# Attention followed by two feed-forward stages: one VectorE instruction for maximum and bias, and the low half of the weights on VectorE

## The chip, the cores and the metric

The kernel runs on one core of one Trainium2 chip. The metric is the device time of one execution in microseconds. Engines are TensorE (PE; its weight loads are PEld), VectorE (DVE), ScalarE (ACT), GpSimd (POOL) and SyncE (SP), which issues most of the transfers.

## The reference, cut to what matters

For each of 4 batches and 8 heads (576 positions, head size 64) q and k are rotated, and then

```python
scores = scale * np.matmul(q_rot, k_rot.transpose(0, 1, 3, 2))
scores = scores - np.max(scores, axis=-1, keepdims=True)
attn = np.exp(scores)
attn = attn / (np.sum(attn, axis=-1, keepdims=True) + 1e-09)
return np.matmul(attn, v).astype(np.float32)
```

The result, 2304 rows of 512, goes through a feed-forward layer (`g = max(0.01 h, h)` between two matrices, 2048 wide), and then each row through one of eight experts (1024 wide, relu), chosen by the largest of eight scaled scores and weighted with its softmax value.

## The kernel before, in words

Products that need more than 16 bits are made of two parts, a high and a low one. For the softmax weights that means: an exponential E in 32 bits, its high part in 16 bits (`a_hi`), and the rest, E minus the high part, again in 16 bits (`a_lo`). Both parts lie side by side in the tile P, which one DMA transposes into PT for the product with v (`a_transpose`, `a_pv`).

Attention is cut into 144 units: 16 pairs of heads, 9 units in each (128 rows of one head; the ninth takes the last 64 rows of both heads). The program is written as a list of steps, one unit entering per step, and the order of all work is the order in which it is issued: each engine takes its instructions in that order. In step i the kernel issues the exponentials of unit i-1, maximum and bias of unit i, high and low part of unit i-1, the scores of unit i+1, and the product with v of unit i-4 (LAG is 4). The same step issues one part of the first feed-forward layer when one is due: `m_s1` and `m_s2` on TensorE, and between them `m_g` (ScalarE), `m_leaky` (VectorE), `m_gh` (ScalarE) and `m_gl` (GpSimd). Then there are pieces of other jobs: decoding the feed-forward matrices, which come as 64-bit numbers (`weights`, `decode`), preparing q, k and v of the next pair (`prep`, `prep_v`), and passing on finished rows (`x_done`, `route`). How many pieces a step takes is set by the planned costs in RATE1 to RATE3, not by time.

The order inside a step is a string of letters. ORDER1 holds until the first part of the feed-forward layer, ORDER2 while matrices are still being decoded beside it, ORDER3 after that:

```python
ORDER1 = 'EXFHfsBLSVGAKhlCx2s'
ORDER2 = 'ESVXsFfGHLAKhlC2xBs'
ORDER3 = 'FESXfHsLGVBKAshlC2x'
```

E is `a_exp`, X `a_max`, B `a_bias`, H `a_hi`, L `a_lo` with the transposing DMA, V `a_pv`, A its evacuation (`a_evac`), F and f `a_fin`, C `a_scores`, S `m_s1`, G `m_g`, K `m_leaky`, h `m_gh`, l `m_gl`, 2 `m_s2`, s and x pieces of other jobs.

Buffers: scores S two (`psS`), E two, P three, PT four, and one each for the feed-forward layer's PSUM tile h (`psH`) and for g. So the next `m_s1` can begin only when `m_leaky` (L279) has read h.

While matrices are being decoded, `a_hi` is an instruction of ScalarE (L528) and `a_bias` too (L515); after that both are VectorE's (L530, L517). `a_max` (L509) is VectorE's and `a_lo` (L534) GpSimd's throughout. After attention come the rest of the feed-forward layer, the choice of experts and the experts' blocks (`e_h`, `e_o`); the diff does not reach them.

Of the kernel before, what the change touches and what calls it, by code (L numbers as in the profile page):

```python
# [9 lines left out]
F32 = mybir.dt.float32  # L10
# [5 lines left out]
AF = mybir.ActivationFunctionType  # L16
ALU = mybir.AluOpType
AX = mybir.AxisListType
# [3 lines left out]
B, H, S, D = 4, 8, 576, 64  # L22
# [4 lines left out]
NBLK = NCH + NE - 1  # L27
NA = NCH - 2
NALWAYS = NCH + 2
LN_P = 10.397207708399179  # L30
EPS_P = 1e-9 * 32768.0
OOB = 8192
LAG = 4
XTB = 2
# [10 lines left out]
CAP = 1.5  # L45
TLOAD = 4
BUR = 1.5
ORDER1 = 'EXFHfsBLSVGAKhlCx2s'
ORDER2 = 'ESVXsFfGHLAKhlC2xBs'
ORDER3 = 'FESXfHsLGVBKAshlC2x'  # L50
SLIM = 1.2
ELOAD = 2
NMERGED = 60
# [48 lines left out]
def attention_moe_kernel(ctx: ExitStack, tc: tile.TileContext, qkv, w_in, w_out, emb, tau, w1, w2,  # L102
                         rope, ident, tokc, iota, pcol, out):
    nc = tc.nc

    def pool(name, bufs=1, **kw):
        return ctx.enter_context(tc.tile_pool(name=name, bufs=bufs, **kw))

    const = pool("const")
    small = pool("small", 3)  # L110
# [14 lines left out]
    enT = const.tile([128, 4, NE], F32, name="enT")  # L125
    junk = const.tile([128, 640], BF16, name="junk")
    itau = const.tile([128, 1], F32, name="itau")
    lnp = const.tile([128, 1], F32, name="lnp")
    half = const.tile([128, 1], F32, name="half")

    def ps_o():
# [43 lines left out]
    xjobs, vjobs, rjobs, wjobs = deque(), deque(), deque(), []  # L175
# [79 lines left out]
    def m_s1(i=None):  # L255

        if not m_ready() or i is not None and not pace(i):
            return None
        j, fs = munits[M.unit]
        M.unit += 1  # L260
        m = Ctx()
        m.j, m.fs, m.h = j, fs, ps_h()
        for f, c0, c1 in fs:
            n = 0
            for a, b_ in ((0, 0), (1, 0), (0, 1)):
                for c in range(4):
                    nc.tensor.matmul(m.h[:, c0:c1], lhsT=wi[:, a, c, 128 * f:128 * f + 128], rhs=xT[j][:, 4 * b_ + c, 0:c1 - c0],  # L267
                                     start=(n == 0), stop=(n == 11))
                    n += 1
        return m  # L270

    def m_g(m):
        m.g = mp.tile([128, 256], F32, name="g", bufs=1)
        for f, c0, c1 in m.fs:
            nc.scalar.activation(out=m.g[:, c0:c1], in_=m.h[:, c0:c1], func=AF.Copy, scale=uw[:, f:f + 1])  # L275

    def m_leaky(m):
        for f, c0, c1 in m.fs:
            nc.vector.scalar_tensor_tensor(out=m.g[:, c0:c1], in0=m.h[:, c0:c1], scalar=uw01[:, f:f + 1], in1=m.g[:, c0:c1], op0=ALU.mult, op1=ALU.max)  # L279
# [75 lines left out]
    pep = at.enter_context(tc.tile_pool(name="pep", bufs=2))  # L355
# [5 lines left out]
    pairs = {}  # L361
# [143 lines left out]
        return ps  # L505

    def a_max(g, u, ps):
        mx = small.tile([128, 2], F32, name="amx")
        nc.vector.tensor_reduce(out=mx[:, 0:1], in_=ps[:, :, 0:288], axis=AX.XY, op=ALU.max)  # L509
        return ps, mx  # L510

    def a_bias(g, u, ps, mx):
        sc = pairs[g][2]
        if any(z.live for z in wjobs):
            nc.scalar.activation(out=mx[:, 1:2], in_=mx[:, 0:1], func=AF.Identity, scale=sc[:, 1:2], bias=lnp)  # L515
        else:
            nc.vector.tensor_scalar(out=mx[:, 1:2], in0=mx[:, 0:1], scalar1=sc[:, 1:2], scalar2=LN_P, op0=ALU.mult, op1=ALU.add)  # L517

    def a_exp(g, u, ps, mx):
        sc = pairs[g][2]  # L520
        e = pep.tile([128, S], F32, name="E")
        nc.scalar.activation(out=e.rearrange("p (a b) -> p a b", a=2), in_=ps[:, :, 0:288], func=AF.Exp, scale=sc[:, 0:1], bias=mx[:, 1:2])  # L522
        return e

    def a_hi(e, i):
        p = pep.tile([128, 2 * S], F16, name="P", bufs=3)
        if i % (HI_ACT if M.unit else HI_A1) == 0 and any(z.live for z in wjobs):
            nc.scalar.activation(out=p[:, 0:576], in_=e, func=AF.Copy)  # L528
        else:
            nc.vector.tensor_copy(out=p[:, 0:576], in_=e)  # L530
        return p

    def a_lo(e, p):
        nc.gpsimd.tensor_tensor(out=p[:, 576:1152], in0=e, in1=p[:, 0:576], op=ALU.subtract)  # L534

    def a_transpose(p):
        pt = ptp.tile([128, 9, 128], F16, name="PT")
        nc.sync.dma_start_transpose(out=pt, in_=p)
        return pt
# [19 lines left out]
    def merged(g, u):  # L559
        return 9 * g + u < NMERGED  # L560

    def a_evac(g, u, o, xo):
        w = 65 if merged(g, u) else 129
        for h, q0, m, ob, oc in pv_parts(g, u):
            nc.scalar.activation(out=xo[ob:ob + m, h, 0:w], in_=o[ob:ob + m, oc:oc + w], func=AF.Copy)  # L565

    def a_fin(g, u, xo):
# [11 lines left out]
        w = 64 if merged(g, u) else 128  # L579
        nc.vector.tensor_scalar(out=rd[r], in0=xo[r, :, w:w + 1], scalar1=EPS_P, scalar2=s3[r, 2:3], op0=ALU.add, op1=ALU.mult)  # L580
        yield
# [71 lines left out]
    nc.sync.dma_start(out=idn, in_=ident)  # L653
    nc.sync.dma_start(out=itau, in_=tau.to_broadcast([128, 1]))
    nc.vector.memset(ones, 2.0)
    nc.vector.memset(lnp, LN_P)
    nc.vector.memset(half, -0.5)
    for i in range(2):
        nc.gpsimd.memset(v16s[i][:, 0:5, :, 128:130], 1.0)
# [74 lines left out]
    def end(g):  # L734
        for _ in g:
            pass
# [235 lines left out]
    units = [(g, u) for g in range(4 * B) for u in range(9)]  # L972
    n = len(units)
    ps_, pt_, xo_ = {}, {}, {}
# [13 lines left out]
    def slot(x=False, must=False):  # L988
        used = dict(A=0.0, V=0.0, G=0.0)
        for z in jobs():  # L990
            p = z.nxt
            if p.x != x or M.step < p.at or M.tick < p.tick or (p.when is not None and not p.when()):
                continue
            if x and L.x == M.tick:
                continue
            if p.must != must:
                continue
            if not p.must and z in wjobs and any(budget[e] <= 0 for e in p.cost):
                continue
            if not p.must and any(used[e] >= SLIM for e in p.cost):  # L1000
                continue
            for e, c in p.cost.items():
                budget[e] -= c
                used[e] += c
            if x:
                L.x = M.tick
            z.begun = True
            z.run()

    def step(i):  # L1010

        M.tick += 1
        M.step = i if i is not None else M.step
        rate = RATE1 if M.unit == 0 else RATE2 if any(z.live for z in wjobs) else RATE3
        for e in budget:
            budget[e] = min(budget[e] + rate[e], BUR * rate[e])
        now = i is not None and 0 <= i < n
        prv = i is not None and 0 <= i - 1 < n
        fin = i is not None and 0 <= i - LAG < n
        slot(must=True)  # L1020
        m = f = None
        for z in ORDER1 if rate is RATE1 else ORDER2 if rate is RATE2 else ORDER3:
            if z == "E" and prv:
                e = a_exp(*units[i - 1], *ps_.pop(i - 1))
            elif z == "S":
                m = m_s1(i)
            elif z == "X" and now:
                ps_[i] = a_max(*units[i], ps_[i])
            elif z == "F" and L.fin and i is not None:
                f = a_fin(*L.fin)  # L1030
                next(f)
                L.fin = None
            elif z == "f" and f:
                end(f)
            elif z == "B" and now:
                a_bias(*units[i], *ps_[i])
            elif z == "H" and prv:
                p = a_hi(e, i)
            elif z == "L" and prv:
                a_lo(e, p)  # L1040
                pt_[i - 1] = a_transpose(p)
            elif z == "V" and fin:
                g, u = units[i - LAG]
                o = a_pv(g, u, pt_.pop(i - LAG))
            elif z == "A" and fin:
                if u % 2 == 0:
                    xo_[g, u // 2] = pep.tile([128, 2, 129], F32, name="xo")
                a_evac(g, u, o, xo_[g, u // 2])
                if u % 2 or u == 8:
                    L.fin = (g, u, xo_.pop((g, u // 2)))  # L1050
            elif z == "G" and m:
                m_g(m)
            elif z == "K" and m:
                m_leaky(m)
            elif z == "h" and m:
                m_gh(m)
            elif z == "l" and m:
                m_gl(m)
            elif z == "C" and i is not None and 0 <= i + 1 < n:
                ps_[i + 1] = a_scores(*units[i + 1])  # L1060
            elif z == "2" and M.q:
                m_s2(M.q.popleft())
            elif z == "x":
                slot(x=True)
            elif z == "s":
                slot()
        if m:
            M.q.append(m)
        if R.late:
            slot()  # L1070
            slot()
# [85 lines left out]
    for i in range(4):  # L1157
# [17 lines left out]
                            in1=cend.unsqueeze(1).to_broadcast([1, NBLK, NE]), op=ALU.is_ge)  # L1175
# [27 lines left out]
    g = gates(0, NCH)  # L1203
# [103 lines left out]
```

## Time and profile before

| | |
|---|---|
| median of 3 runs | 1080.92 us (1079.94 to 1080.98) |
| the profiled execution | 1080.7 us, of which the span is 1078.9 us |
| TensorE busy | 956.0 us (89%) |
| VectorE busy | 790.2 us (73%) |
| ScalarE busy | 716.5 us (66%) |
| GpSimd busy | 563.3 us (52%) |
| `a_max` L509 | 144 instructions, 107.7 us |
| `a_lo` L534 | 144 instructions, 204.3 us |
| `a_exp` L522 | 144 instructions, 118.2 us |

The span runs from the first to the last instruction. A share over the whole span mixes stages with different limits, so the stages are looked at one by one. A mean duration well above an instruction's shortest one means that it was held while it ran.

### The profile page before, as it was taken

The numbers are of one execution on the slowest core, as the hardware profiler recorded it, in microseconds if no ns is written. First come the engines' busy times: TensorE is split into PE (matmuls) and PEld (weight loads), VectorE is DVE, ScalarE is ACT, GpSimd is POOL, SyncE is SP. The second block draws the span as 40 slices with busy tenths as digits, with TensorE's granted clock in tenths as the row PEclk, the third lists the DMA queues.
The fourth block names the chain that finished last, engine by engine and source line by source line (L and its number), as shares of the span: only waits on it lengthen the run. The fifth ranks groups of instructions, "written<-read, shape, count | busy, mean of one in ns | idle before, by whom it ended". The sixth has DMA issues, their size and how long they took to land. (4 is left out here: it accounts for less than half of the span.)

```text
span 1078.9 us, 19752 instructions
## 1 busy us (share of the span) xinstructions
PE 956.0 (89%) x6737; PEld 710.9 (66%) x6737; DVE 790.2 (73%) x1472; ACT 716.5 (66%) x1404; POOL 563.3 (52%) x558
## 2 busy tenths in 40 slices
PE   1666666988999999999998999999999899999996
PEld 1333333765667767677776677788877678888885
DVE  7898899886798763776976855312376999998992
ACT  7988888987556635455664554435345888888883
POOL 2577756776678663786777756422232361211111
PEclk9999999998999999999999999999999999999999
DMA  8979987965868853388588474301152111115190
GB/s 227 197 181 203 221 179 165 209 142 126 171 95 140 185 108 71 73 152 168 86 163 150 89 120 81 60 16 40 30 176 98 40 59 40 50 50 195 34 340 21
DMA packets 273611, 133.54 MB, mean 124 GB/s; under 512 B 244951, under 2 KB 253399, under 8 KB 273504
## 3 DMA queue, kind: packets, MB, share of 16 engines
q1 hardware_dynamic: 270304, 122.24, 52.0%
q0 software_dynamic: 3200, 9.97, 2.8%
q8 instruction: 55, 0.90, 0.3%
q14 instruction: 52, 0.43, 0.1%
HBM read 120.04 MB, written 10.49 MB: 121 GB/s over the span
## 5 line engine op out<-in xcount | busy, mean ns | idle before, releaser
L534 POOL TENSOR_TENSOR P<-E,P 128x576 f16<-128x576 f32 x144 | 204.3, 1419 | 63.7 <-DVE P L530 29.5
L267 PE MATMUL h<-xT,wi 128*128 128x256 f16 (+1 forms) x1920 | 216.7, 265 | 20.5 <-DVE g L279 12.1
L267 PEld LDWEIGHTS <-wi 128*128 128x128 f16 x1920 | 168.7, 100 | 64.4 <-issue 47.0
L287 POOL TENSOR_TENSOR gl<-g,gh 128x256 fp32r<-128x256 f32 x144 | 119.5, 830 | 147.3 <-ACT gh L283 141.5
L298 PE MATMUL acc<-wo,gh 128*128 128x512 f32 x576 | 196.4, 422 | 0.0
L279 DVE SCALAR_TENSOR_TENSOR g<-h,uw,g 128x256 f32<-128x256 f32 (+1 forms) x160 | 71.2, 453 | 141.0 <-ACT g L275 138.8
L275 ACT ACTIVATE g<-h,uw 128x256 f32<-128x256 f32 (+1 forms) x160 | 70.2, 449 | 136.8 <-PE h L267 117.5
L555 PE MATMUL o<-v,PT 128*128 128x65 f16 (+3 forms) x1770 | 102.8, 215 | 42.9 <-ACT xo L565 32.4
L555 PEld LDWEIGHTS <-PT 128*128 128x128 f16 (+1 forms) x1770 | 93.4, 111 | 55.6 <-issue 39.0
L503 PE MATMUL S<-stk 128*128 128x288 f16 (+1 forms) x320 | 105.4, 329 | 26.7 <-ACT E L522 25.7
L522 ACT ACTIVATE E<-S,amx,sc 128x576 f32<-128x576 f32 x144 | 118.2, 821 | 4.8 <-DVE amx L517 4.0
L283 ACT ACTIVATE gh<-g 128x256 fp32r<-128x256 f32 x144 | 60.0, 417 | 84.2 <-DVE g L279 83.6
L298 PE MATMUL acc<-wo,gl 128*128 128x512 f32 x288 | 115.6, 401 | 0.1
L298 PEld LDWEIGHTS acc<-wo,gh 128*128 128x128 f32 x576 | 98.5, 191 | 26.1 <-issue 0.2
L509 DVE TENSOR_REDUCE amx<-S 128x1 f32<-128x576 f32 x144 | 107.7, 748 | 1.4 <-PE S L504 1.1
L944 POOL DMA_INDIRECT out<-eo,idi x18 | 25.7, 1430 | 154.1 <-ACT eo L942 153.4
L504 PE MATMUL S<-stk 64*128 64x288 f16 (+1 forms) x320 | 105.9, 331 | 0.0
L504 PEld LDWEIGHTS <-stk 64*128 64x128 f16 (+1 forms) x320 | 31.2, 98 | 86.3 <-issue 64.4
L391 POOL TENSOR_TENSOR t<-raw,tab 128x320 f32<-128x320 f32 x62 | 64.1, 1054 | 7.4 <-DMA raw<-in_qkv 7.4
L530 DVE CAST P<-E 128x576 f16<-128x576 f32 x90 | 50.9, 565 | 19.9 <-ACT E L522 18.9
L298 PEld LDWEIGHTS acc<-wo,gl 128*128 128x128 f32 x288 | 54.9, 191 | 14.1 <-POOL gl L287 1.5
L426 DVE SCALAR_TENSOR_TENSOR stg<-raw,ps,stg 128x320 f16<-128x320 f32 x64 | 57.7, 941 | 0.0
(239 smaller groups left out, 1956.5 us busy)
## 6 DMA issues: line engine op xcount, KB each, us to landing
rb<-in_w SPq DMA_DIRECT2D x78, 512.0 KB
ra<-in_w SPq DMA_DIRECT2D x76, 512.0 KB
raw<-in_qkv SPq DMA_DIRECT2D x15, 640.0 KB
raw<-in_w_in SPq DMA_DIRECT2D x16, 512.0 KB
raw<-in_w_out SPq DMA_DIRECT2D x16, 512.0 KB
raw<-in_qkv SPq DMA_DIRECT2D x18, 320.0 KB
x2s<-x SPq DMA_DIRECT2D x18, 256.0 KB
v<-v SPq DMA_DIRECT2D x16, 162.5 KB
```

The costliest lines, as they stand in the source:

```text
L267: nc.tensor.matmul(m.h[:, c0:c1], lhsT=wi[:, a, c, 128 * f:128 * f + 128], rhs=xT[j][:, 4 * b_ + c, 0:c1 - c0], start=(n == 0), stop=(n == ...
L275: nc.scalar.activation(out=m.g[:, c0:c1], in_=m.h[:, c0:c1], func=AF.Copy, scale=uw[:, f:f + 1])
L279: nc.vector.scalar_tensor_tensor(out=m.g[:, c0:c1], in0=m.h[:, c0:c1], scalar=uw01[:, f:f + 1], in1=m.g[:, c0:c1], op0=ALU.mult, op1=ALU.max)
L287: nc.gpsimd.tensor_tensor(out=m.gl, in0=m.g, in1=m.gh.bitcast(F32), op=ALU.subtract)
L298: nc.tensor.matmul(M.acc[t], lhsT=g_[:, tt], rhs=wo[:, a, f], start=(f == 0 and n == 0), stop=(f == NF - 1 and n == 2))
L391: eng.tensor_tensor(out=t2[t][:, :, :, o:o + 32], in0=raw[:, t, :, :, i:i + 32], in1=sn[:, :, o:o + 32].unsqueeze(1).to_broadcast([128, 2, ...
L503: nc.tensor.matmul(ps[o:o + m, n, 0:288], lhsT=stk[:, h, c0:c0 + m], rhs=stk[:, 2 + h, ks], start=True, stop=False)
L504: nc.tensor.matmul(ps[o:o + m, n, 0:288], lhsT=stk[hr, h, c0:c0 + m], rhs=stk[hr, 4, ks], start=False, stop=True)
L509: nc.vector.tensor_reduce(out=mx[:, 0:1], in_=ps[:, :, 0:288], axis=AX.XY, op=ALU.max)
L522: nc.scalar.activation(out=e.rearrange("p (a b) -> p a b", a=2), in_=ps[:, :, 0:288], func=AF.Exp, scale=sc[:, 0:1], bias=mx[:, 1:2])
L534: nc.gpsimd.tensor_tensor(out=p[:, 576:1152], in0=e, in1=p[:, 0:576], op=ALU.subtract)
L555: nc.tensor.matmul(o[ob:ob + m, oc + z:oc + z + w], lhsT=pt[:, i, q0:q0 + m], rhs=v16[:, i, h, c:c + w], start=(n == 0), stop=(n == len(to ...
```

## The change

Maximum and bias become one VectorE instruction: it multiplies the scores in PSUM by minus the scale, writes the products into E (where the exponentials overwrite them later), and gives their minimum, which is the bias. `a_bias` and its letter B go. The factor 2**15, which was in the bias as its logarithm, is now applied when the weights are parted: `a_hi` multiplies E by it, and `a_lo` computes E times the factor minus the high part in one VectorE instruction; it was a GpSimd subtraction. E is taken from its pool one step earlier.

```diff
-LN_P = 10.397207708399179
-EPS_P = 1e-9 * 32768.0
+P_UP = 32768.0
+EPS_P = 1e-9 * P_UP
...
-ORDER1 = 'EXFHfsBLSVGAKhlCx2s'
-ORDER2 = 'ESVXsFfGHLAKhlC2xBs'
-ORDER3 = 'FESXfHsLGVBKAshlC2x'
+ORDER1 = 'EXFHfsLSVGAKhlCx2s'
+ORDER2 = 'ESVXsFfGHLAKhlC2xs'
+ORDER3 = 'FESXfHsLGVKAshlC2x'
...
     def a_max(g, u, ps):
-        mx = small.tile([128, 2], F32, name="amx")
-        nc.vector.tensor_reduce(out=mx[:, 0:1], in_=ps[:, :, 0:288], axis=AX.XY, op=ALU.max)
-        return ps, mx
-
-    def a_bias(g, u, ps, mx):
+
+        mx = small.tile([128, 1], F32, name="amx")
+        e = pep.tile([128, S], F32, name="E")
+        nc.vector.tensor_scalar(out=e.rearrange("p (a b) -> p a b", a=2), in0=ps[:, :, 0:288], scalar1=pairs[g][2][:, 1:2], scalar2=None, op0=ALU.mult, op1=ALU.min, accum_out=mx)
+        return ps, mx, e
+
+    def a_exp(g, u, ps, mx, e):
         sc = pairs[g][2]
-        if any(z.live for z in wjobs):
-            nc.scalar.activation(out=mx[:, 1:2], in_=mx[:, 0:1], func=AF.Identity, scale=sc[:, 1:2], bias=lnp)
-        else:
-            nc.vector.tensor_scalar(out=mx[:, 1:2], in0=mx[:, 0:1], scalar1=sc[:, 1:2], scalar2=LN_P, op0=ALU.mult, op1=ALU.add)
-
-    def a_exp(g, u, ps, mx):
-        sc = pairs[g][2]
-        e = pep.tile([128, S], F32, name="E")
-        nc.scalar.activation(out=e.rearrange("p (a b) -> p a b", a=2), in_=ps[:, :, 0:288], func=AF.Exp, scale=sc[:, 0:1], bias=mx[:, 1:2])
+        nc.scalar.activation(out=e.rearrange("p (a b) -> p a b", a=2), in_=ps[:, :, 0:288], func=AF.Exp, scale=sc[:, 0:1], bias=mx)
         return e
...
-            nc.scalar.activation(out=p[:, 0:576], in_=e, func=AF.Copy)
+            nc.scalar.activation(out=p[:, 0:576], in_=e, func=AF.Copy, scale=P_UP)
         else:
-            nc.vector.tensor_copy(out=p[:, 0:576], in_=e)
+            nc.vector.tensor_scalar(out=p[:, 0:576], in0=e, scalar1=P_UP, scalar2=None, op0=ALU.mult)
         return p
 
     def a_lo(e, p):
-        nc.gpsimd.tensor_tensor(out=p[:, 576:1152], in0=e, in1=p[:, 0:576], op=ALU.subtract)
+        nc.vector.scalar_tensor_tensor(out=p[:, 576:1152], in0=e, scalar=P_UP, in1=p[:, 0:576], op0=ALU.mult, op1=ALU.subtract)
```

## Rows read from the trace of the kernel before

**Rows 1.** The page: span, and busy time of each engine.

```profile
span 1078.9 us, 19752 instructions
PE 956.0 (89%) x6737; PEld 710.9 (66%) x6737; DVE 790.2 (73%) x1472; ACT 716.5 (66%) x1404; POOL 563.3 (52%) x558
```

**Rows 2.** Busy time in four stretches; last columns: granted clock, DMA share, GB/s.

```profile
22.00:187.00 165.00, 102.43 (x729) 55.61 (x729) 145.75 (x252) 139.03 (x287) 111.45 (x91) 1.00 0.86 192
187.00:270.00 83.00, 75.02 (x637) 52.81 (x634) 66.05 (x126) 69.98 (x157) 60.59 (x55) 0.94 0.76 158
270.00:690.00 420.00, 403.35 (x3209) 296.16 (x3209) 293.59 (x669) 229.45 (x534) 288.55 (x318) 1.00 0.66 122
690.00:1079.00 389.00, 371.08 (x2158) 304.09 (x2155) 269.22 (x393) 262.30 (x397) 98.40 (x86) 0.99 0.25 84
```

**Rows 3.** Groups of VectorE instructions, 22 to 187 us: busy us, mean ns | idle before.

```profile
L195 DVE SCALAR_TENSOR_TENSOR raw<-raw 128x512 uint32<-128x512 uint32 x19 | 20.3, 1072 | 4.2 <-ACT raw L193 3.6 <-issue 0.7
L197 DVE SCALAR_TENSOR_TENSOR raw<-raw 128x512 uint32<-128x512 uint32 x20 | 20.2, 1008 | 0.2
L396 DVE TENSOR_TENSOR raw<-raw,tab 128x640 f32<-128x640 f32 x10 | 16.3, 1633 | 10.9 <-POOL t L391 9.3 <-ACT amx L515 1.5
...
L487 DVE SCALAR_TENSOR_TENSOR v<-raw,ps,v 128x320 f16<-128x320 f32 x8 | 12.6, 1617 | 0.3 <-ACT v L484 0.3
L233 DVE SCALAR_TENSOR_TENSOR wi<-raw,ps,wi 128x512 f16<-128x512 f32 x11 | 12.4, 1128 | 0.0
```

**Rows 4.** The same instructions by tile, whole span: shortest/median/longest in ns.

```profile
L396 DVE TENSOR_TENSOR raw<-raw,tab x32: 814/1442/1916, 6.0 to 602.2; 128x640 f32<-128x640 f32 x32
L487 DVE SCALAR_TENSOR_TENSOR v<-raw,ps,v x32: 540/556/4397, 15.0 to 624.5; 128x320 f16<-128x320 f32 x32
L195 DVE SCALAR_TENSOR_TENSOR raw<-raw x32: 676/832/1778, 15.9 to 257.6; 128x512 uint32<-128x512 uint32 x32
L197 DVE SCALAR_TENSOR_TENSOR raw<-raw x32: 665/694/1780, 16.6 to 261.4; 128x512 uint32<-128x512 uint32 x32
...
L233 DVE SCALAR_TENSOR_TENSOR wi<-raw,ps,wi x16: 732/912/1781, 26.4 to 264.1; 128x512 f16<-128x512 f32 x16
```

**Rows 5.** Timeline of VectorE (first row) and GpSimd, 152 to 157 us.

```profile
152.12 4.87 DVE L487 SCALAR_TENSOR_TENSOR v<-raw,ps,v 128x320 f16<-128x320 f32 x2
...
152.88 1.27 POOL L534 TENSOR_TENSOR P<-E,P 128x576 f16<-128x576 f32 x1
154.12 1.28 POOL L212 TENSOR_TENSOR wo<-raw,wo 128x512 fp32r<-128x512 f32 x1
155.36 1.27 POOL L534 TENSOR_TENSOR P<-E,P 128x576 f16<-128x576 f32 x1
```

**Rows 6.** GpSimd's low part, 22 to 187 us (groups); SP's wait for it, 30 to 187 us (waits).

```profile
L534 POOL TENSOR_TENSOR P<-E,P 128x576 f16<-128x576 f32 x38 | 55.4, 1461 | 12.1 <-issue 6.5 <-ACT P L528 3.2 <-DMA raw<-in_qkv 1.8
...
SPq L538 <- POOL P L534: 46.0, 23, 3.8
```

**Rows 7.** Maximum, bias and high part by tile; shortest/median/longest in ns.

```profile
L530 DVE CAST P<-E x90: 428/460/1824, 271.5 to 679.0; 128x576 f16<-128x576 f32 x90
...
L509 DVE TENSOR_REDUCE amx<-S x144: 736/746/759, 22.7 to 673.7; 128x1 f32<-128x576 f32 x144
...
L517 DVE TENSOR_SCALAR amx<-amx,sc x89: 197/204/209, 272.3 to 674.8; 128x1 f32<-128x1 f32 x89
L515 ACT ACTIVATE amx<-amx,lnp,sc x55: 369/373/388, 24.6 to 267.9; 128x1 f32<-128x1 f32 x55
```

**Rows 8.** Nearest prices: a TENSOR_SCALAR from PSUM (by tile), ScalarE's accumulator read (groups).

```profile
L309 DVE TENSOR_SCALAR x<-acc,ux x8: 735/751/752, 278.0 to 819.5; 128x512 f32<-128x512 f32 x8
...
L386 ACT ACTIVATION_READ_ACCUMULATOR junk<-raw 128x1 f32 x48 | 9.4, 195 | 0.0
```

**Rows 9.** Waits, 270 to 690 us: us in total, times, longest us.

```profile
DVE g L279 <- ACT g L275: 64.8, 49, 3.9
...
PE h L267 <- DVE g L279: 9.0, 10, 2.5
```

More of the change, by code (lines that the diff above doesn't have):

```diff
@@ L127, in attention_moe_kernel @@
     itau = const.tile([128, 1], F32, name="itau")
-    lnp = const.tile([128, 1], F32, name="lnp")
     half = const.tile([128, 1], F32, name="half")
@@ L655, in attention_moe_kernel @@
     nc.vector.memset(ones, 2.0)
-    nc.vector.memset(lnp, LN_P)
     nc.vector.memset(half, -0.5)
@@ L1034, in step @@
                 end(f)
-            elif z == "B" and now:
-                a_bias(*units[i], *ps_[i])
             elif z == "H" and prv:
```

## The prediction, made before the changed kernel was run

> **What bounds the kernel now.** I read the page first, for the span and the totals [rows 1]: TensorE is busy 89%, VectorE 73%, but that is a mean over unlike stages. The busy times by stretch tell them apart [rows 2]. The reader should see four. A, 22 to 187 us: attention beside the decoding of the matrices, without the feed-forward layer; VectorE is busy 145.75 of 165 us, TensorE only 102. B, 187 to 270: the first feed-forward parts join; TensorE 75 of 83, VectorE 66. C, 270 to 690: TensorE 403 of 420, VectorE 294. D, 690 to the end: nothing of the change runs there, and I count it as 0. So VectorE sets the time in A and TensorE in C. The DMA share is 0.86 in A, not full.
>
> Then I asked what fills VectorE in A. Its groups there [rows 3] have means far above the shortest durations of the same instructions [rows 4]: L487 takes 1617 ns against 540, L396 1633 against 814. The timeline shows why [rows 5]: two L487 began at 152.12 and were through only after 4.87 us, while three GpSimd instructions ran back to back until 156.63; VectorE stood until the last had ended. Instructions from PSUM show nothing of the kind: `a_max` takes 736 to 759 ns in all 144 cases [rows 7]. So GpSimd holds up VectorE instructions that work in SBUF. Count times (mean minus shortest) over the five groups gives 7.5 (L195) + 6.9 (L197) + 8.2 (L396) + 8.6 (L487) + 4.4 (L233) = 35.6 us of holding in A [rows 3, 4]. `a_lo` makes up 55.4 of GpSimd's 111.45 us there [rows 2, 6].
>
> **The change part by part.** *Low part on VectorE.* GpSimd loses 1.46 us per unit in A [rows 6]. On VectorE, L233 is the same operation on the same types, 512 wide and with a scalar per partition: 732 ns at the shortest; L195, with a constant, 676 [rows 4]. Between L487 and L233 the slope is 192 ns for 192 elements, so 576 wide costs 740 (constant) to 796 ns. The new one has a constant: I take 0.74 us.
>
> The Trainium skill (Vector Engine (DVE) Microarchitecture Reference, Points that are easy to get wrong) says that an instruction of this family with two SBUF sources that are not both bf16 runs at half rate. L233 has two such sources and took 732 ns for 512 elements [rows 4], one element in little over 1 ns, so the row does not bear the rule out. By the rule the sum would be rival 4's.
>
> *Maximum and bias in one.* The nearest row is L309, a TENSOR_SCALAR from PSUM, 512 wide: 751 ns [rows 8]; 64 elements more make it 0.815 us. What reading the accumulated minimum costs no VectorE row shows. Nothing at the least; at the most what ScalarE's read takes, 195 ns [rows 8]. Against 0.746 for the reduction [rows 7] that is +0.07 to +0.26; I take +0.17. It reads PSUM, so I expect it to be held as little as L309 (735 to 752 ns).
>
> The Trainium skill (VectorE: DVE Perf Modes, Two Vector instructions with no wait between them) counts an operation that also writes out its accumulator as two instructions. By that the upper end would hold: 0.09 us more in each of 144 units, 13 us of VectorE, of which A would show 3.
>
> *Bias removed.* In A and B that frees ScalarE of 0.373 us per unit, in C VectorE of 0.204 [rows 7]. *High part.* A multiplication in place of a cast, same sizes; I keep 0.46 us in C and ScalarE's time in A. *E taken earlier.* The new instruction overwrites what `a_lo` two units before has read; that is now VectorE's own earlier work, so no wait is added.
>
> *Transfer and queues.* The transposing DMA is still issued by SP after the low part. SP waited 46.0 us in A for GpSimd's low part [rows 6]; now it waits for VectorE's, which stands behind the pieces of other jobs in the step, and behind the DMA in SP's queue stand matrix loads and the transposes of q and k. PT is wanted four units later, so I count nothing; without that cover each late transpose would stop TensorE.
>
> *New order on VectorE.* `a_lo` stands ahead of `m_leaky`. `m_leaky` frees the only h buffer, so all that delays it delays the next `m_s1`. In C this wait is 9.0 us now, in ten places [rows 9]. In B `a_lo` also waits for ScalarE's high part, queued after `m_g`.
>
> **The sum, stretch by stretch.** A, 38 units. VectorE without holding: 145.75 - 35.6 = 110.2. New work: 38 x (0.74 + 0.17) = 34.6. Holding: GpSimd keeps 56.05 of 111.45 us, so half, 17.9, stays for the old instructions; a low part meets GpSimd busy in 56 of 165 us and waits half of a mean instruction (56.05 us by 91 - 38 = 53 gives 1.06, half is 0.53): 38 x 0.34 x 0.53 = 6.8. Together 169.5. VectorE's idle time is 19.25 us; of this 9.3 was for a GpSimd product and 1.5 for the bias on ScalarE [rows 3], which I let go, and keep 8.4. That makes 178, so +13. The relief is (35.6 - 17.9 - 6.8) / 38 = 0.29 us per unit.
>
> B, 16 units: +16 x 0.91 = 14.6, less 16 x 0.29 = 4.6, so VectorE has 76 of 83 us, as much as TensorE. I take +2, between -3 and +10 (all of the net 10).
>
> C, 90 units: 90 x (0.74 + 0.17 - 0.204) = 63.5, less 90 x 0.29 = 26: VectorE goes from 294 to 331 of 420. TensorE's work hides this. VectorE's idle time falls from 126 to 89, and 64.8 of it is waiting for `m_g` [rows 9], which shrinks first. I let the 9.0 us that TensorE waits for `m_leaky` grow as that idle time shrinks, 9.0 x (126 / 89 - 1) = +4. Bounds: -9, if the wait goes away with GpSimd's holding, and +64, if the cover fails altogether.
>
> Sum: 13 + 2 + 4 = +19 on the profiled execution's 1080.7 (span 1078.9 and 1.8 around it; the median of the runs is 0.2 more): 1099.5, so **1100 us**.
>
> **Rivals.** (1) *Faster: holding collapses.* Place: VectorE in A. What counts is how often GpSimd's instructions follow each other without a gap, as at 152.88 to 156.63 [rows 5]; with half of its work gone that may nearly end. With 5 us of holding in place of 24.7, and the new maximum at its lower price (-3.8), A takes 154 (-11); with -2 in B and -5 in C: 1063. It decides once holding in A falls below 165 - 144.8 - 8.4 = 12 us. Against it: the low part is itself one more instruction that can be held.
>
> (2) *VectorE becomes the bound in C.* If a third of the 0.71 us added per unit shows in each, because VectorE's step no longer ends before TensorE's, C costs 21 in place of 4, and B 5: 1120. For it: `m_leaky` waits behind everything. Against it: 89 us of idle time left.
>
> (3) *No difference.* Holding in A comes out near 12 us, and B and C cancel: 1081.
>
> (4) *The halving.* The low part takes one more 576 elements' time, 0.6 us: A +23, B +10, and a third of C's 54: 1151. L233 speaks against it.
>
> **How the numbers follow.** Chances: forecast 0.46 (its own range 1086 to 1112), rival 1 0.22, rival 2 0.20, rival 3 0.10, rival 4 0.02. The range for 8 in 10 reaches into rival 1 and past rival 2: 1066 to 1124; about half of rival 1 lies below, some of rival 2 and all of rival 4 above. A measurement of this kernel tells 0.2%, some 2 us, from no change. Faster: rival 1, 0.22. Within: rival 3, 0.10. Slower: the rest, 0.68.
>
> **What would show it.** The new instruction at L509's place: 0.82 to 1.01 us, hardly spread. The low part: 0.74 us at the shortest, mean some 0.9 in A. L195, L197, L396, L487 and L233 in A: about half of the excess gone. VectorE over 90% busy in the stretch that answers to A, and that stretch some 13 us longer; ScalarE's bias gone. In C: TensorE's wait for `m_leaky` somewhat above 9 us. D unchanged. The prediction is wrong if stretch A gets shorter, which would mean that holding fell more than GpSimd's busy time, or if C grows by more than 10 us.

## The result, and the profile after

The changed kernel takes 1070.63 us (median of 4 runs), the kernel before 1080.43 in the same comparison: a ratio of 0.9909, with a 95% interval of 0.9892 to 0.9926. It is 10 us faster. The forecast was 1100; what came is nearest to rival 1.

The page of the changed kernel, span and busy times, against [rows 1]:

```profile
span 1068.2 us, 19714 instructions
PE 956.1 (90%) x6737; PEld 710.7 (67%) x6737; DVE 825.6 (77%) x1670; ACT 701.0 (66%) x1349; POOL 366.3 (34%) x414
```

VectorE has 35 us more to do than before, GpSimd 197 less. The stretches that answer to [rows 2] (columns as there; the borders are moved with the start of the same units):

```profile
22.00:179.00 157.00, 103.11 (x733) 55.59 (x734) 143.92 (x329) 127.43 (x249) 59.34 (x53) 1.00 0.90 203
179.00:265.00 86.00, 75.55 (x633) 53.13 (x630) 70.14 (x160) 65.42 (x141) 35.04 (x39) 0.94 0.78 155
265.00:680.00 415.00, 403.19 (x3217) 295.63 (x3213) 326.81 (x758) 230.03 (x534) 169.46 (x228) 1.00 0.66 123
680.00:1068.00 388.00, 370.24 (x2155) 304.11 (x2153) 269.01 (x393) 262.33 (x397) 98.13 (x86) 1.00 0.25 84
```

The reader is to see the first row. VectorE has taken over 38 low parts and its busy time fell all the same, from 145.75 to 143.92 us, and the stretch with it by 8. Its groups there, against [rows 3] (busy us, mean ns | idle before; the edits move line numbers, so L194 here is L195 before, and the low part, L534 before, is L527):

```profile
L510 DVE TENSOR_SCALAR_CACHE_REDUCE E<-S,sc 128x576 f32<-128x576 f32 x39 | 31.5, 807 | 0.0
L527 DVE SCALAR_TENSOR_TENSOR P<-E,P 128x576 f16<-128x576 f32 x38 | 31.4, 828 | 2.2 <-ACT P L521 2.2
L196 DVE SCALAR_TENSOR_TENSOR raw<-raw 128x512 uint32<-128x512 uint32 x20 | 17.1, 856 | 0.0
L194 DVE SCALAR_TENSOR_TENSOR raw<-raw 128x512 uint32<-128x512 uint32 x19 | 13.8, 728 | 0.2 <-ACT raw L192 0.2
L232 DVE SCALAR_TENSOR_TENSOR wi<-raw,ps,wi 128x512 f16<-128x512 f32 x11 | 11.4, 1039 | 0.1
L425 DVE SCALAR_TENSOR_TENSOR stg<-raw,ps,stg 128x320 f16<-128x320 f32 x20 | 11.4, 611 | 0.0
L395 DVE TENSOR_TENSOR raw<-raw,tab 128x640 f32<-128x640 f32 x10 | 10.7, 1075 | 6.8 <-POOL t L390 6.8
L486 DVE SCALAR_TENSOR_TENSOR v<-raw,ps,v 128x320 f16<-128x320 f32 x8 | 7.0, 908 | 0.0
...
L405 DVE SCALAR_TENSOR_TENSOR sc<-m 128x1 f32<-128x1 f32 x5 | 2.0, 404 | 0.2
...
L469 DVE COPY stg<-stg 128x640 f16<-128x640 f16 x5 | 1.6, 317 | 0.0
```

Counted as in the prediction, against the shortest durations of [rows 4], the five groups are now held for 1.0 + 3.8 + 2.6 + 2.9 + 3.4 = 13.7 us; it was 35.6. At least three more groups, which the prediction did not count, were held as well. The same view of the kernel before, 22 to 187 us:

```profile
L426 DVE SCALAR_TENSOR_TENSOR stg<-raw,ps,stg 128x320 f16<-128x320 f32 x20 | 15.1, 794 | 0.0
...
L406 DVE SCALAR_TENSOR_TENSOR sc<-m 128x1 f32<-128x1 f32 x5 | 4.0, 803 | 0.2
...
L470 DVE COPY stg<-stg 128x640 f16<-128x640 f16 x5 | 3.8, 751 | 0.0
```

Their means fell to 611, 404 and 317 ns: 20 x 0.183 + 5 x 0.399 + 5 x 0.434 = 7.8 us of holding less.

To compare stretches between kernels I use the start of the exponentials of units 38, 54 and 143 (the 39th, 55th and 144th instruction of that line in the timeline), in us of the profiled executions, one of each kernel:

| kernel | unit 38 | unit 54 | unit 143 | span | 38 to 54 | 54 to 143 |
|---|---|---|---|---|---|---|
| before | 188.4 | 268.3 | 678.2 | 1078.9 | 79.9 | 409.9 |
| changed | 180.2 | 263.6 | 668.0 | 1068.2 | 83.4 | 404.4 |
| changed, again | 181.3 | 263.6 | 668.1 | 1068.4 | 82.3 | 404.5 |
| low part alone | 181.6 | 266.9 | 671.3 | 1072.7 | 85.3 | 404.4 |
| maximum and bias alone | 188.7 | 268.5 | 679.7 | 1079.7 | 79.8 | 411.2 |
| GpSimd reads added, early | 208.2 | 291.7 | 701.5 | 1102.3 | 83.5 | 409.8 |
| GpSimd writes added, early | 182.7 | 264.7 | 675.0 | 1075.2 | 82.0 | 410.3 |
| GpSimd reads added, late | 180.0 | 262.0 | 702.2 | 1102.9 | 82.0 | 440.2 |
| low part of the matrix | 179.9 | 261.5 | 666.0 | 1066.3 | 81.6 | 404.5 |
| leaky first, ORDER2 | 181.6 | 261.0 | 667.0 | 1067.3 | 79.4 | 406.0 |
| high part on VectorE | 179.6 | 259.2 | 664.5 | 1064.8 | 79.6 | 405.3 |
| leaky first, ORDER3 | 180.9 | 264.1 | 665.0 | 1065.3 | 83.2 | 400.9 |
| both in ORDER2's stretch | 180.9 | 262.5 | 668.2 | 1068.6 | 81.6 | 405.7 |
| high part, and ORDER3 | 181.4 | 260.8 | 663.8 | 1064.1 | 79.4 | 403.0 |

So the change gains 8.2 us up to unit 38, loses 3.5 up to unit 54, gains 5.5 up to unit 143, and leaves the rest as it was (400.7 us before, 400.2 after). The same kernel run twice differs by 1.1 us in a stretch, so smaller differences between rows say nothing.

### The profile page after: what moved, and what is told of

Same layout as the page of the kernel before. It is cut to its first block, busy times and chain, and to the rows that moved or that the text cites. A ratio compares the mean times of both kernels' runs of the same rounds, so it can differ in the third digit from the quotient of the medians.

```text
span 1068.2 us, 19714 instructions
## 1 busy us (share of the span) xinstructions
PE 956.1 (90%) x6737; PEld 710.7 (67%) x6737; DVE 825.6 (77%) x1670; ACT 701.0 (66%) x1349; POOL 366.3 (34%) x414
## 5 line engine op out<-in xcount | busy, mean ns | idle before, releaser
L286 POOL TENSOR_TENSOR gl<-g,gh 128x256 fp32r<-128x256 f32 x144 | 112.9, 784 | 329.7 <-ACT gh L282 304.2
L274 ACT ACTIVATE g<-h,uw 128x256 f32<-128x256 f32 (+1 forms) x160 | 70.1, 449 | 123.6 <-PE h L266 115.4
L527 DVE SCALAR_TENSOR_TENSOR P<-E,P 128x576 f16<-128x576 f32 x144 | 119.8, 832 | 17.8 <-ACT P L521 15.4
L510 DVE TENSOR_SCALAR_CACHE_REDUCE E<-S,sc 128x576 f32<-128x576 f32 x144 | 116.4, 808 | 2.3 <-PE S L503 2.0
L390 POOL TENSOR_TENSOR t<-raw,tab 128x320 f32<-128x320 f32 x62 | 66.4, 1098 | 8.3 <-DMA raw<-in_qkv 8.3
L523 DVE TENSOR_SCALAR P<-E 128x576 f16<-128x576 f32 x90 | 52.8, 586 | 18.6 <-ACT E L515 16.9
L502 PEld LDWEIGHTS <-stk 128*128 128x128 f16 (+1 forms) x320 | 33.6, 105 | 33.6 <-issue 12.8
```

The lines of the kernel that those rows point to most:

```text
L286: nc.gpsimd.tensor_tensor(out=m.gl, in0=m.g, in1=m.gh.bitcast(F32), op=ALU.subtract)
L502: nc.tensor.matmul(ps[o:o + m, n, 0:288], lhsT=stk[:, h, c0:c0 + m], rhs=stk[:, 2 + h, ks], start=True, stop=False)
L510: nc.vector.tensor_scalar(out=e.rearrange("p (a b) -> p a b", a=2), in0=ps[:, :, 0:288], scalar1=pairs[g][2][:, 1:2], scalar2=None, op0=AL ...
L527: nc.vector.scalar_tensor_tensor(out=p[:, 576:1152], in0=e, scalar=P_UP, in1=p[:, 0:576], op0=ALU.mult, op1=ALU.subtract)
```

## The experiments

### Each half of the change by itself

The low part alone, in the kernel before:

```diff
-        nc.gpsimd.tensor_tensor(out=p[:, 576:1152], in0=e, in1=p[:, 0:576], op=ALU.subtract)
+        nc.vector.scalar_tensor_tensor(out=p[:, 576:1152], in0=e, scalar=1.0, in1=p[:, 0:576], op0=ALU.mult, op1=ALU.subtract)
```

> The kernel before with one edit: the low part is a VectorE instruction (factor 1.0); maximum, bias and high part as before. Theory H (holding): the gain comes from GpSimd's low part no longer holding VectorE; then this edit alone gives most of it, 1068 to 1075 us, and the five VectorE groups of the stretch up to unit 38 lose at least 15 of their 35.6 us of holding. Theory S (ScalarE's relief): the gain comes from the bias leaving ScalarE, which no longer waits for the maximum; then this edit gives none, 1080 us or more, since VectorE only gets more to do.

Maximum and bias in one alone, in the changed kernel:

```diff
-P_UP = 32768.0
+P_UP = 1.0
...
-        nc.vector.scalar_tensor_tensor(out=p[:, 576:1152], in0=e, scalar=P_UP, in1=p[:, 0:576], op0=ALU.mult, op1=ALU.subtract)
+        nc.gpsimd.tensor_tensor(out=p[:, 576:1152], in0=e, in1=p[:, 0:576], op=ALU.subtract)
```

> The changed kernel with the low part back on GpSimd as a subtraction; the factor 2**15 is left out, so the weights are not scaled and the output differs in its last digits. It keeps maximum and bias in one instruction. H: 1077 to 1086 us, the holding of the five groups stays at 30 us or more. S: 1069 to 1074 us. If both contribute, each of these two runs gives a part and the parts add up to about 10 us.

The low part alone took 1076.35 us, 0.9971 of the kernel before (0.9957 to 0.9985); maximum and bias alone 1081.6 us, 1.0016 (1.0003 to 1.003). The changed kernel, run again beside later experiments, took 1070.77 us, 0.9925 (0.9912 to 0.9938).

> The changed kernel once more, so that the other runs of this call can be read against it on the same chip: 0.988 to 0.994 of the kernel before.

VectorE's five groups up to unit 38 (busy us, mean ns | idle before), with the low part alone, 22 to 180 us:

```profile
L197 DVE SCALAR_TENSOR_TENSOR raw<-raw 128x512 uint32<-128x512 uint32 x20 | 15.9, 793 | 0.0
L195 DVE SCALAR_TENSOR_TENSOR raw<-raw 128x512 uint32<-128x512 uint32 x19 | 14.8, 781 | 1.1 <-ACT raw L193 1.1
L233 DVE SCALAR_TENSOR_TENSOR wi<-raw,ps,wi 128x512 f16<-128x512 f32 x11 | 11.0, 1004 | 0.4 <-ACT wi L231 0.4
L396 DVE TENSOR_TENSOR raw<-raw,tab 128x640 f32<-128x640 f32 x10 | 10.8, 1076 | 5.9 <-POOL t L391 4.2 <-ACT amx L515 1.7
...
L487 DVE SCALAR_TENSOR_TENSOR v<-raw,ps,v 128x320 f16<-128x320 f32 x8 | 7.0, 909 | 0.0
```

and with maximum and bias alone, 22 to 187 us:

```profile
L196 DVE SCALAR_TENSOR_TENSOR raw<-raw 128x512 uint32<-128x512 uint32 x20 | 19.0, 948 | 0.2
L194 DVE SCALAR_TENSOR_TENSOR raw<-raw 128x512 uint32<-128x512 uint32 x19 | 18.6, 982 | 1.4 <-ACT raw L192 1.4
...
L395 DVE TENSOR_TENSOR raw<-raw,tab 128x640 f32<-128x640 f32 x10 | 15.2, 1524 | 8.2 <-POOL t L390 8.2
L232 DVE SCALAR_TENSOR_TENSOR wi<-raw,ps,wi 128x512 f16<-128x512 f32 x11 | 13.3, 1213 | 0.0
L486 DVE SCALAR_TENSOR_TENSOR v<-raw,ps,v 128x320 f16<-128x320 f32 x8 | 11.9, 1526 | 0.0
```

Theory S falls: the merged instruction alone gains nothing, and without the low part's move the five groups stay held for 31.8 us (5.8 + 5.7 + 7.1 + 7.9 + 5.3). With the low part alone their holding falls to 13.2 us (2.0 + 2.6 + 2.6 + 3.0 + 3.0), as much as in the changed kernel, and unit 38 begins 6.8 us earlier. But H expected 1068 to 1075 and missed: it took the low part for nearly the whole. By the ratios the halves give -3.1 and +1.7 us, and the change run again -8.1; they don't add up: some 6.7 us of the gain come only with both. The table places part of this between units 38 and 54, 85.3 us with the low part alone and 82.3 to 83.4 with both. The waits of VectorE with the low part alone, 180 to 265 us, show what stands there:

```profile
DVE P L534 <- ACT P L528: 18.2, 13, 3.5
```

The low part waits for ScalarE's high part, 18.2 us there and 13.1 in the changed kernel (below), where ScalarE no longer has the bias to do. So, as far as the table shows, taking the bias from ScalarE is worth something only once VectorE waits for ScalarE; this is argued from the waits, and no run takes away the bias alone. By the table's spans the low part alone gains 6.2 us, by the medians 3.1. That comes from the executions that were profiled: with the low part alone 1075.0 us, 1.35 below its median, and the kernel before 1080.7, 1.1 above the median it was compared with; and 2.3 us of the first lie outside the span, against 1.8. Where the rest of the missing sum lies is open.

### GpSimd's holding, put back by itself

In the changed kernel, GpSimd work that nothing depends on: first two subtractions per unit that read SBUF, then four memsets. Both kernels give the low part of g one buffer instead of two, to make room.

```diff
+    scr = const.tile([128, 256], F32, name="scr")
...
-        m.gl = mp.tile([128, 256], F32R, name="gl")
+        m.gl = mp.tile([128, 256], F32R, name="gl", bufs=1)
...
     def a_lo(e, p):
         nc.vector.scalar_tensor_tensor(out=p[:, 576:1152], in0=e, scalar=P_UP, in1=p[:, 0:576], op0=ALU.mult, op1=ALU.subtract)
+        if M.unit == 0:
+            tb = tab.rearrange("p a c d -> p (a c d)")
+            for _ in range(2):
+                nc.gpsimd.tensor_tensor(out=scr, in0=tb[:, 0:256], in1=tb[:, 256:512], op=ALU.subtract)
```

> The changed kernel, and in each unit before the first feed-forward part two GpSimd subtractions of 256 columns on the rotation table into a scratch tile that nobody reads (some 0.72 us each by the low part of g, so as much GpSimd time as the old low part took); the low part of g has one buffer instead of two, to make room, which does not matter before the feed-forward parts start. Nothing depends on the added work. H: the stretch from 22 us to unit 38, 157 us in the changed kernel, grows by 15 to 35 us, with VectorE's five groups held again by 25 us or more; the whole takes 1085 to 1105 us. S, or a theory that the transfer of the weights left earlier: within 3 us of the changed kernel's 1070.

```diff
+        if M.unit == 0:
+            for _ in range(4):
+                nc.gpsimd.memset(scr, 0.0)
```

> As the run with the added GpSimd subtractions, but four GpSimd memsets of the scratch tile per unit instead, so GpSimd is busy without reading. H with the holding tied to what GpSimd reads: the stretch up to unit 38 stays within 4 us of 157, the whole within 4 us of 1070. H with the holding tied to GpSimd being busy at all: the stretch grows in proportion to the memsets' time, by 10 us or more if they take 1 us per unit.

With the subtractions the whole takes 1104.13 us (one execution). The stretch up to unit 38, and VectorE's groups in it (the added lines move the numbers again; L528 is the low part here):

```profile
22.00:207.00 185.00, 102.95 (x736) 55.68 (x736) 172.90 (x327) 129.42 (x249) 132.85 (x129) 1.00 0.77 172
```

```profile
L528 DVE SCALAR_TENSOR_TENSOR P<-E,P 128x576 f16<-128x576 f32 x38 | 39.6, 1043 | 0.2 <-ACT P L522 0.2
...
L195 DVE SCALAR_TENSOR_TENSOR raw<-raw 128x512 uint32<-128x512 uint32 x19 | 17.6, 927 | 0.7 <-POOL scr L532 0.7
L197 DVE SCALAR_TENSOR_TENSOR raw<-raw 128x512 uint32<-128x512 uint32 x19 | 16.7, 877 | 0.0
L426 DVE SCALAR_TENSOR_TENSOR stg<-raw,ps,stg 128x320 f16<-128x320 f32 x20 | 15.6, 820 | 0.0
L396 DVE TENSOR_TENSOR raw<-raw,tab 128x640 f32<-128x640 f32 x10 | 13.7, 1368 | 8.8 <-POOL t L391 8.8
L233 DVE SCALAR_TENSOR_TENSOR wi<-raw,ps,wi 128x512 f16<-128x512 f32 x11 | 11.7, 1064 | 0.0
L487 DVE SCALAR_TENSOR_TENSOR v<-raw,ps,v 128x320 f16<-128x320 f32 x8 | 9.1, 1182 | 0.0
```

VectorE's list of work is the same as in the changed kernel. Yet it is busy 172.9 us in place of 143.9, and the stretch is 28 us longer. The five groups are held for 23.1 us (25 or more was expected), and the low parts more than in the changed kernel: 38 x (1.043 - 0.741) = 11.5 us. GpSimd's added work came out longer than meant, 0.99 us each.

With the memsets, the stretch and GpSimd's costliest group in it:

```profile
22.00:181.00 159.00, 102.84 (x727) 55.27 (x727) 143.02 (x329) 127.30 (x248) 102.89 (x206) 1.00 0.90 199
```

```profile
L531 POOL MEMSET scr<- 128x256 f32 x152 | 47.5, 313 | 7.1
```

GpSimd is busy 102.9 of 159 us, nearly its 111.45 of before [rows 2], and VectorE is held no more than in the changed kernel: it is busy 143.0 us, against 143.9. The stretch grew by 2.5, inside the 4 that were expected. One small group is an exception: the copies L470, five instructions with one SBUF input, have a mean of 642 ns here and 317 in the changed kernel, 1.6 us in all. But for these, it is not GpSimd's being busy that holds VectorE, but its reading. The Trainium skill (SBUF — State Buffer, Who interferes with whom) says this: a VectorE instruction with two SBUF inputs contends with a GpSimd instruction that reads SBUF, not with one that only writes, and the later one is blocked whole. These two runs bear out the first half; the 4.87 us of [rows 5] fit the second. The whole took 1077.1 us (one execution), 3 more than expected: units 54 to 143, where nothing was added, took 410.3 us, and 409.8 with the early subtractions, against 404.4. I put that down to the one buffer, which both runs have; no run has it alone.

### The same holding under TensorE

The changed kernel with the subtractions only after decoding has ended, units 54 to 143 (the edit is shown against the run with the early subtractions):

```diff
-        if M.unit == 0:
+        if not any(z.live for z in wjobs):
```

> The changed kernel with the two added GpSimd subtractions per unit on the rotation table only after decoding has ended (units 54 to 143), none before; the low part of g has one buffer, as in the two earlier runs with added GpSimd work, whose units 54 to 143 took 409.8 and 410.3 us without it (404.4 in the changed kernel). Theory H for the third stretch too: VectorE's SBUF instructions are held again (L426 of before goes from 0.54 back to 0.8 us or more in the mean), TensorE waits more often for the leaky maximum, and the stretch takes 414 to 430 us. Rival: TensorE is the bound there and hides the holding; then 408 to 412, and the gain of 5.5 us in that stretch came from elsewhere.

It took 1104.69 us (one execution), and units 54 to 143 took 440.2 us, 30 more than with one buffer and no added work there. That is above what H expected and far from the rival. TensorE's waits between 265 and 700 us, and a VectorE group there:

```profile
PE h L267 <- DVE g L279: 23.3, 21, 4.0
```

```profile
L426 DVE SCALAR_TENSOR_TENSOR stg<-raw,ps,stg 128x320 f16<-128x320 f32 x36 | 27.1, 790 | 0.0
```

TensorE is the busiest engine there and hides little of this: it waits for the leaky maximum, which stands behind the held instructions. All its waits there come to 35 us, against 13 with one buffer and no added work, so that some 21 of the 30 us are waits. The other 9 are TensorE's own work, busy 404.7 us (262 to 702 us) where the two other runs have 395 to 396 for as many instructions; its mean granted clock was 0.98 there and 0.99 in those. Some of the waits may be GpSimd's own queue, whose low part of g comes later (TensorE waited 2.5 us for it).

### Taking the mechanism one step further

In the changed kernel, the low part of the second feed-forward matrix on VectorE:

```diff
-                nc.gpsimd.tensor_tensor(out=wo[:, 1, f], in0=r, in1=wo[:, 0, f].bitcast(F32), op=ALU.subtract)
+                nc.vector.tensor_tensor(out=wo[:, 1, f], in0=r, in1=wo[:, 0, f].bitcast(F32), op=ALU.subtract)
```

> The changed kernel with one more GpSimd subtraction given to VectorE: the low part of the second feed-forward matrix (16 times, 1.5 us on GpSimd, 10 of them up to unit 38). If GpSimd's holding is still worth more than the work: VectorE gets 10 x 0.6 to 0.7 = 6 to 7 us more in the stretch up to unit 38 and loses the some 8.6 us of holding that lies under these ten instructions, so that the stretch gains 0 to 3 us and the whole 0 to 4. If the work decides: 3 to 7 us slower.

It took 1070.26 us, 0.9927 (0.9911 to 0.9944), where the changed kernel has 0.9925: no difference. Up to unit 38 VectorE's ten new instructions are busy 8.1 us, and yet its busy time is 142.9 us, against 143.9. What VectorE was held under these instructions and what they cost it cancel.

### The stretch that got longer, and the order

VectorE's waits in the changed kernel, 179 to 265 us:

```profile
DVE P L527 <- ACT P L521: 13.1, 11, 2.7
```

Two edits, each by itself, and then together. The first puts the low part behind the leaky maximum; the second gives the high part of this stretch to VectorE:

```diff
-ORDER2 = 'ESVXsFfGHLAKhlC2xs'
+ORDER2 = 'ESVXsFfGHAKLhlC2xs'
```

> The changed kernel with one edit in ORDER2, the order of the stretch between the first feed-forward part and the end of decoding: the low part is issued behind the leaky maximum instead of ahead of it. Theory: that stretch got longer (from unit 38 to unit 54: 79.9 us before, 83.4 in the changed kernel) because VectorE stands in the low part waiting for ScalarE's high part (13.1 us) with the leaky maximum queued behind. Then the stretch comes back to 80 to 82 us and the whole gains 1.5 to 3.5 us on the changed kernel. Rival: the stretch is longer because TensorE, busy 75.6 of 86 us, and VectorE simply have no room; then nothing changes, within 1 us.

```diff
-HI_ACT = 1
+HI_ACT = 1000
```

> The changed kernel with one edit: in that same stretch the high part is VectorE's (0.46 us) instead of ScalarE's. It takes away the wait for ScalarE in another way and adds 16 x 0.4 = 6 us of VectorE. If the wait for ScalarE's high part is what costs: 80 to 83 us from unit 38 to 54, with little left of the wait, though the high part then waits for ScalarE's exponential. If VectorE's busy time is what costs there: 86 us or more.

> The changed kernel with both edits of the second stretch: leaky maximum ahead of the low part, and the high part on VectorE. If both take away the same wait, no more than either alone: 79 to 80 us from unit 38 to 54 and 1066 to 1068 us. If each takes away something of its own: 76 to 78 us and 1063 to 1065.

Leaky maximum first: 1067.6 us, 0.9894 (0.9878 to 0.9909), 79.4 us from unit 38 to 54. High part on VectorE: 1067.02, 0.989 (0.9873 to 0.9906), 79.6 us. Both stretches are a little shorter than expected. The wait for ScalarE's high part is gone from VectorE's waits in both, so it was what the stretch had lost, not a lack of room; with the high part on VectorE it is busy 82.6 us between 179 and 265 us, against 70.1, and the stretch is shorter all the same. Together they take 1070.69 us, 0.9915 (0.9899 to 0.9932), and 81.6 us: worse than either, which neither expectation had. TensorE's largest wait in that stretch is then 6.3 us in three places for a small VectorE instruction (L95); but with the leaky maximum first alone it was 5.5, so this does not explain it. The cause stays open.

The same change of order later:

```diff
-ORDER3 = 'FESXfHsLGVKAshlC2x'
+ORDER3 = 'FESXfHsGVKLAshlC2x'
```

> The changed kernel with one edit in ORDER3: the low part is issued behind the leaky maximum. TensorE waits 7.3 us for it between 265 and 680 us. If the low part ahead of it is what it waits for, most of that goes and units 54 to 143 take 399 to 403 us in place of 404.4; if the wait comes from pieces of other jobs, nothing changes, within 1 us.

It took 1067.18 us, 0.9883 (0.9859 to 0.9908); units 54 to 143 take 400.9 us, inside what was expected. But TensorE's wait for the leaky maximum only goes from 7.3 to 5.1 us, where most of it was to go; its wait for the exponential goes from 2.7 to 1.2, another 1.5 us.

Last, the high part on VectorE and the later order together:

> The changed kernel with the two edits that each gained in a stretch of its own: the high part on VectorE while decoding goes on beside the feed-forward parts (unit 38 to 54: 79.6 us alone, against 82.3 to 83.4), and the leaky maximum ahead of the low part in ORDER3 (units 54 to 143: 400.9 us alone, against 404.4). If the stretches stand apart, the gains add: 1063 to 1065 us. If what is saved in one is lost in the next, as when both edits of ORDER2 were put together (405.7 us afterwards): 1067 us or more.

It took 1063.95 us, 0.9848 (0.9832 to 0.9864): faster than the changed kernel and some 16 us faster than before, as the sum of the two gains would have it. The execution in the table was the slowest of five (1065.86 us); units 54 to 143 took 403.0 us in it, not 400.9. TensorE's waits between 262 and 680 us:

```profile
PE h L266 <- DVE g L278: 4.4, 8, 1.1
```

## Why the prediction was wrong

**The step that failed** is the holding in stretch A: "GpSimd keeps 56.05 of 111.45 us, so half, 17.9, stays for the old instructions". The price was scaled with GpSimd's busy time. The row of before that it was made from [rows 5] showed something else, three GpSimd instructions in a row, under which VectorE stood for the sum of all three. Without the low parts such rows are rarer: by the timelines, three and more GpSimd instructions with less than 0.1 us between them filled 79 us of stretch A before (13 rows) and 30 us in the changed kernel (5 rows). Holding fell faster than busy time, too: to 13.7 us in the five groups with 53% of GpSimd's time left, and for the low part itself to 38 x (0.828 - 0.741) = 3.3 in place of 6.8. That the rows are the reason is argued; no run changes them alone. The shortest low part, by tile (shortest/median/longest in ns):

```profile
L527 DVE SCALAR_TENSOR_TENSOR P<-E,P x144: 741/759/1366, 30.5 to 669.7; 128x576 f16<-128x576 f32 x144
```

The larger fault is that only five groups were counted; three others gave back 7.8 us more, which the sum kept as VectorE's own work.

Of the 29 us between forecast and result stretch A makes 21 (+13 forecast, -8.2 measured) and stretch C 9.5.

**Sizes that were off.** For VectorE's busy time in A 169.5 us was predicted and 143.9 measured. Of the difference, the old holding makes 4.2 us, the uncounted groups 7.8, and the low part's own holding 3.5. Then the new work: VectorE's instructions overlap, so a duration is more than an instruction takes from its neighbours. The timeline of the changed kernel (start, us):

```profile
71.53 0.74 DVE L527 SCALAR_TENSOR_TENSOR P<-E,P 128x576 f16<-128x576 f32 x1
72.20 0.68 DVE L194 SCALAR_TENSOR_TENSOR raw<-raw 128x512 uint32<-128x512 uint32 x1
72.80 0.81 DVE L510 TENSOR_SCALAR_CACHE_REDUCE E<-S,sc 128x576 f32<-128x576 f32 x1
73.54 0.08 DVE L510 DVE_READ_ACCUMULATOR E<-S,sc 128x1 f32 x1
73.54 0.22 DVE L573 TENSOR_SCALAR rd<-xo,ps 64x2 f32<-64x2 f32 x1
```

and of the kernel before:

```profile
231.97 0.75 DVE L509 TENSOR_REDUCE amx<-S 128x1 f32<-128x576 f32 x1
232.63 0.68 DVE L197 SCALAR_TENSOR_TENSOR raw<-raw 128x512 uint32<-128x512 uint32 x1
```

From start to start the low part takes 0.67 us (I took 0.74), and the merged instruction 0.74 against 0.66 for the reduction: +0.08, where I took +0.17. That is 38 x 0.16 = 6 us. These four make 21.6 of the 25.6 us; the rest I did not place. Idle time was 13.1 in place of 8.4: the wait for a GpSimd product, which the sum let go, is still 6.8 us (L395 above). So A took 157 us, not 178.

**The accumulator.** The Trainium skill (VectorE: DVE Perf Modes, Two Vector instructions with no wait between them) was right on the form: the read is an instruction of its own, 0.08 us. But the next instruction starts with it, at 73.54, so that the upper end of my price did not hold. What the Trainium skill (Vector Engine (DVE) Microarchitecture Reference, Points that are easy to get wrong) says of two SBUF sources did not hold for the low part: 741 ns at the shortest for 576 elements, as I had priced it. (The prediction's "one element in little over 1 ns" for L233 is a misreading: 732 ns for 512 elements are 1.43 each; 1 ns per element is the slope between L487 and L233.)

**Stretch B** (+2 forecast, between -3 and +10) came out at +2.4 to +3.5, and by a mechanism that the prediction named: the low part waits for ScalarE's high part with the leaky maximum behind it. Two experiments take just that away. The +2 itself was luck: it was taken from VectorE being as full as TensorE, with 76 us of work, and VectorE was busy 70.1 of 86.

**Stretch C** (+4 forecast, -9 the lower bound) came out at -5.5, and here too the step was wrong: VectorE's busy time rose by 33 us, where I had 37, but I let TensorE's wait for the leaky maximum grow as VectorE's idle time shrank, and it fell from 9.0 [rows 9] to 7.3. TensorE's other larger waits of before, 270 to 690 us:

```profile
PE S L503 <- ACT E L522: 4.2, 5, 1.5
PE h L267 <- DVE xsq L611: 2.0, 2, 1.0
```

and those of the changed kernel, 265 to 680 us:

```profile
PE h L266 <- DVE g L278: 7.3, 9, 2.0
PE S L502 <- ACT E L515: 2.7, 4, 0.8
```

The wait for L611 is gone. Together that is 1.7 + 1.5 + 2.0 = 5.2 us, nearly the whole gain. So it is not VectorE's load that makes TensorE wait there. That it is single long delays on VectorE is argued from groups like L426, whose mean fell from 1097 ns to 538. VectorE groups, before (270 to 690 us), then changed (265 to 680 us):

```profile
L426 DVE SCALAR_TENSOR_TENSOR stg<-raw,ps,stg 128x320 f16<-128x320 f32 x36 | 38.1, 1097 | 0.0
```

```profile
L425 DVE SCALAR_TENSOR_TENSOR stg<-raw,ps,stg 128x320 f16<-128x320 f32 x36 | 18.0, 538 | 0.0
```

The run with added late reads shows the other direction: there the mean is 790 ns again, and TensorE's wait 23.3 us.

**The rivals.** Rival 1 named the place (holding of VectorE in A) and nearly the sizes in A and C: -11, -2 and -5 against -8.2, +3.5 and -5.5; in B not even the sign. Its point of decision, less than 12 us of holding, was wrong with the prices it stood on: 13.7 + 3.3 = 17 us were enough. Rival 2 did not come, rival 4 neither. Stretch D stayed as it was.

## What to carry to other kernels

Where an instruction's mean stands well above its shortest duration, count that excess over all groups of the engine: it is not work, and it may go away whole with the engine that causes it. Before giving work to a full VectorE, compare its price there, from start to start, with what GpSimd's version takes from VectorE by holding it. And look at what the moved instruction now stands in front of: about half of the further gain here (0.989 to 0.9848, of 0.9925 to 0.9848) came from putting it behind the one that TensorE waits for.

## What I had not expected

GpSimd is held in turn. In the changed kernel a GpSimd product of 64 rows and 128 columns, which takes 0.39 us at the shortest (L583 by tile), took 1.97. Timeline of GpSimd in the changed kernel:

```profile
74.09 1.97 POOL L583 TENSOR_TENSOR x<-xo,rd 64x128 f32<-64x128 f32 x1 [2.83 <-DVE rd L575]
```

VectorE's instructions of that time (L194 at 74.46, the low part at 75.06) took no longer than usual, 0.68 and 0.75 us. And TensorE, busy 403 of 415 us, hid little of the holding that was added under it: VectorE's busy time between 54 and 143 rose by some 35 us, for 164 us of GpSimd reads, and the stretch by 30.
